# Late products with v on four tiles of TensorE instead of two, and whole copies of their probabilities

## The chip, the cores and the metric

One core of a Trainium2 chip. The metric is the device time of one execution in microseconds (us). The kernel before takes 708.42 us, the median of three runs (708.2 to 708.72). The engines are named as in the profile: PE is TensorE, PEld its weight loads, DVE is VectorE, ACT is ScalarE, POOL is GpSimd, SP is SyncE, which issues most of the transfers.

## The reference

Chunked attention with 8 memory keys, then a gated feed-forward on all tokens. Batch 4, 8 heads, 768 tokens, head size 64; chunks of 32 queries, each with 8 memory keys and 16 + 32 + 8 keys around it.

```python
for c in range(nc):
    k_full = np.concatenate([mem_k, k[:, :, l_start:r_end]], axis=2)   # 8 + up to 56 keys
    v_full = np.concatenate([mem_v, v[:, :, l_start:r_end]], axis=2)
    scores = scale * np.matmul(q_c, k_full.transpose(0, 1, 3, 2))
    scores = scores - np.max(scores, axis=-1, keepdims=True)
    a = np.exp(scores)
    a = a / (np.sum(a, axis=-1, keepdims=True) + 1e-09)
    out[:, :, c_start:c_end] = np.matmul(a, v_full)
...
rms = np.sqrt(np.mean(x * x, axis=-1, keepdims=True) + 1e-06)
xn = x / rms * rms_g
g = xn @ w_gate
silu = g * (1.0 / (1.0 + np.exp(-g)))
val = xn @ w_val
return (silu * val @ w_out).astype(np.float32)
```

x has 3072 tokens of 512 values (all heads side by side); the feed-forward is 1536 wide.

## The kernel before

**Blocks and units.** The tokens are worked in 8 blocks of 384 (half a batch element). A unit of attention is a block and a pair of heads: 12 chunks of 32 queries for two heads, 32 units in all. The first 8 units (early) and the first two blocks' feed-forward follow an order written out by hand. The other 24 units (late) are worked in 12 pairs, in between the feed-forward of the blocks ahead of them.

**The feed-forward.** For each of 12 slices f of the width, TensorE computes `pg` (gate) and `pv` (value) in 12 matmuls each, and then `po` (out) of the slice before in 9. Each product is made in three passes, with high and low parts of both operands (`xh`, `xl`, `hh`, `hl`, `wh`, `wl`). ScalarE does tanh (L451) and the cast `hh` (L162), VectorE the rest of the gating (L446, L455, L458) and `hl` (L467). TensorE's feed-forward matmuls of the late part stay in the order in which they are written, and so do the matmuls of the visits.

**Visits.** After `pg` or after `pv` of certain slices, given by a table, a visit (`late_steps`) issues attention work. A visit knows a pair `old`, whose probabilities are ready, and a pair `cur`, whose scores are to be made:

- `pT`: three transposes of 128x128 for each unit of `old` (`stage_p`), into two different banks of PSUM
- the copies of `pT` into `pt` (even unit) and `qp` (odd unit) in SBUF (`stage_c`)
- `s`: the scores of `cur` (`stage_s2`), tiles of 64 rows by 32 columns, for two units
- max, subtraction (VectorE), exponential (ScalarE) of `cur`
- `o`: the products of `old` with v (`stage_o`), then copies into `xT` and squares `sq` on ScalarE, their sum on VectorE (`late_r`)
- in every second visit the norm of a block begins (`late_n`): `sh` and `sl`, high and low part of the sum of squares, and later `ssum`, two matmuls with ones
- sums, reciprocals and products with `r` for `cur` (`stage_d`), which make the probabilities of the next visit's `old`

In the first block with visits, the step with `ssum` stands right after the next `pg`; in the later blocks a `pv` and more lie between. Parts of the visits have high priority and the scheduler sets the order on VectorE and ScalarE from there; each engine then works in that fixed order.

**Chunks and rows.** v is laid out with 128 rows for a pair of chunks: 64 keys of the even chunk, then 64 of the odd one. A transposed tile of probabilities has the same rows. Each row half is a chunk's keys, and its columns are that chunk's queries only. The kernel before wants one matmul with all 128 rows for the queries of both chunks, 64 columns, so each row half needs zeros in the columns of the other chunk: the tiles `pt` and `qp` are 768 wide, zeroed once by POOL (L122), and the copies write each row half to its own columns only. They are therefore four copies of 64x384 for a pair of units, two by ScalarE for the lower rows, two by VectorE for the upper.

Of the kernel before, what the change touches and what calls it, by code (L numbers as in the profile page):

```python
# [8 lines left out]
F32 = mybir.dt.float32  # L9
# [4 lines left out]
AF = mybir.ActivationFunctionType  # L14
ALU = mybir.AluOpType
# [5 lines left out]
CH = 32  # L21
# [3 lines left out]
P = 128  # L25
NG = H // 2
HT = 384
NT = HT // P
NC = HT // CH
NJ = NC // 2  # L30
# [4 lines left out]
NE = NG * 2  # L35
WP = 2 * KC - LC - RC
KN, VN = NJ * WP, NJ * 2 * D
# [33 lines left out]
def tile_kernel(ctx: ExitStack, tc: tile.TileContext, q, k, v, w_gate, w_val, w_out, rms_g, out):  # L71
    nc = tc.nc
    const = ctx.enter_context(tc.tile_pool(name="const", bufs=1))
    p1 = ctx.enter_context(tc.tile_pool(name="p1", bufs=1))
# [28 lines left out]
    def on_pe(ins):  # L103
        if pinned:
            tc.keep_in_program_order(ins)

    def psum_a(name):
        return psa.tile([P, 512], F32, name=name, tag="at")

    def psum_m(tag, name):  # L110
        return psm.tile([P, 512], F32, name=name, tag=tag)
# [4 lines left out]
    units = [(b, hf, g) for b in range(B) for hf in range(2) for g in range(NG)]  # L116
    st = {}
    pts = [early.tile([P, NT, 4, 2, CH], F32, name=f"pt{i}") for i in range(2)]
    late = {}

    def zeros(t):
        nc.gpsimd.memset(t, 0.0)  # L122
        return t

    def late_buffers(i):

        if i:
            t = p1.tile([P, HT + VN], F32, name="qp1", tag="A")
            late["q", 1], late["pt", 1] = t[:, 0:HT], zeros(t[:, HT:])
            late["kv", 1] = p1.tile([P, KN + VN], F32, name="kv1", tag="B")  # L130
        else:
            late["q", 0] = p1.tile([P, HT], F32, name="q0", tag="q")
            late["pt", 0] = zeros(p1.tile([P, VN], F32, name="pt0", tag="wy"))
            late["kv", 0] = p1.tile([P, KN + VN], F32, name="kv0", tag="ws")
        late["pt", i] = late["pt", i].rearrange("p (i a s q) -> p i a s q", i=NT, a=4, s=2)

    def load_qk(u):
        d = st.setdefault(u, {})
        if u < NE:
            d["q"] = early.tile([P, HT], F32, name=f"q{u}", tag=f"q{u % 6}")  # L140
            t = early.tile([P, KN], F32, name=f"k{u}", tag=f"k{u % 6}")
            nc.sync.dma_start(out=d["q"], in_=q[u])
        else:

            t = late["kv", u % 2][:, 0:KN]
            d["q"] = late["q", u % 2]
            nc.sync.dma_start(out=d["q"], in_=q[u])
        d["k"] = t.rearrange("p (j k) -> p j k", j=NJ)
        nc.sync.dma_start(out=t, in_=k[u])
# [5 lines left out]

    def pt_of(u):

        return pts[u % 2] if u < NE else late["pt", u % 2]

    def copy(e, out, in_):  # L160
        if e == "a":
            return nc.scalar.copy(out, in_)  # L162
        if e == "g":
            return nc.gpsimd.tensor_copy(out=out, in_=in_)
        return nc.vector.tensor_copy(out=out, in_=in_)  # L165
# [22 lines left out]
    def stage_s2(pair):  # L188

        for u in pair:  # L190
            st[u]["s"] = psum_a(f"s{u}")
        for i in range(NT):
            for cp in range(2):
                for par in range(2):
                    c, o = 4 * i + 2 * par + cp, (2 * i + cp) * KC
                    for u in pair:
                        d = st[u]
                        for e in range(2):
                            r, a = slice(64 * e, 64 * e + 64), 64 * par + CH * (e ^ u % 2)
                            on_pe(nc.tensor.matmul(d["s"][a:a + CH, o:o + KC], lhsT=d["q"][r, c * CH:c * CH + CH],  # L200
                                                   rhs=d["k"][r, c // 2, 40 * cp:40 * cp + KC], start=True, stop=True))

    def stage_m(u):
        stage_ma(u)
        stage_mb(u)
# [20 lines left out]
    def stage_e(u):  # L226
        pe = st[u]["p"]
        nc.scalar.activation(pe, pe, AF.Exp, scale=0.125)

    def stage_d(u):  # L230
        stage_da(u)
        stage_db(u)
# [25 lines left out]
    def stage_p(u, tag=None):  # L258
        d = st[u]
        t = psum_m(tag, f"pT{u}") if tag else psum_a(f"pT{u}")  # L260
        pe = d["p"].rearrange("p j k -> p (j k)")
        for i in range(NT):
            on_pe(nc.tensor.transpose(out=t[:, i * P:(i + 1) * P], in_=pe[:, i * P:(i + 1) * P], identity=ident))  # L263
        d["t"] = t

    def stage_c(u):
        stage_ch(u, 0, "a")
        stage_ch(u, 1, "d")

    def stage_ch(u, hh, e):  # L270
        r = slice(64 * hh, 64 * hh + 64)
        t4 = st[u]["t"][:, 0:HT].rearrange("p (i a q) -> p i a q", i=NT, q=CH)
        copy(e, pt_of(u)[r, :, :, hh, :], t4[r])

    def stage_o(u, tag=None):

        pt, vw = pt_of(u), st[u]["v"]
        o = psum_m(tag, f"o{u}") if tag else psum_a(f"o{u}")
        for j in range(NJ):
            for hh in range(2):  # L280
                on_pe(nc.tensor.matmul(o[64 * hh:64 * hh + 64, j * D:(j + 1) * D], lhsT=vw[:, j, hh],  # L281
                                 rhs=pt[:, j // 2, 2 * (j % 2) + (hh ^ (u % 2 if u >= NE else 0))].rearrange("p c q -> p (c q)"),
                                 start=True, stop=True))
        st[u]["o"] = o[:, 0:HT]

    def late_r(u, x):

        g = units[u][2]
        o = st.pop(u)["o"]
        nc.scalar.copy(x[:, g], o)  # L290
        s = obuf(f"sq{u}")[:, 0:HT]
        nc.scalar.activation(s, x[:, g], AF.Square)
        if g:
            nc.vector.tensor_tensor(out=s, in0=s, in1=late["ss"], op=ALU.add)
        late["ss"] = s

    def late_n(x):

# [191 lines left out]
    def obuf(name):  # L490
        return p3.tile([P, DM], F32, name=name, tag="stg")
# [59 lines left out]
    def last_of(eng):  # L551
        return next(i for i in reversed(nc.cur_bb.bb.instructions) if i.engine == eng.engine)
# [3 lines left out]
    def late_steps():  # L556


        pairs = [(u, u + 1) for u in range(NE, len(units), 2)]
        for n in range(len(pairs) + 1):  # L560
            old = pairs[n - 1] if n else ()
            cur = pairs[n] if n < len(pairs) else ()
            new = pairs[n + 1] if n + 1 < len(pairs) else ()
            for u in old[0:1]:
                if u % NG == 0:
                    late_x["x"] = p1.tile([P, NKT, HT], F32, name="xT", tag="x")
            x = late_x.get("x")
            with tc.high_priority():
                for i, u in enumerate(old):
                    stage_p(u, None if i else "g")  # L570
                for u in old:
                    stage_c(u)
            if not cur:
                yield "p"
            with tc.high_priority():
                if cur:
                    stage_s2(cur)
                for u in cur:
                    stage_m(u)
                for u in cur:  # L580
                    stage_e(u)
                for i, u in enumerate(old):
                    stage_o(u, "v" if cur and i else None)
                for u in old:
                    late_r(u, x)
            norm = late_n(x) if n and n % 2 == 0 else ()
            if norm:
                with tc.high_priority():
                    next(norm)
            with tc.high_priority():  # L590
                for i, u in enumerate(cur):
                    if norm and i:
                        with tc.issue_after(last_of(nc.vector)):
                            stage_d(u)
                    else:
                        stage_d(u)
            for u in new:
                load_qk(u)
            for u in cur if n else ():
                load_v(u)  # L600
            yield "v"
            for _ in norm:
                yield "n"

    def tok_R(n):
        late_buffers(0)
        load_qk(NE)
        load_v(NE)
# [5 lines left out]
    sq = [xq[:, i] for i in range(4)]  # L614
# [35 lines left out]
    def tok_in(w):  # L650
        def fn(n):
            b, f = SEQ[n]
            sp[w, n] = moe_in(w, f, xs01[b])
        return fn
# [28 lines left out]
    def tok_o(n):  # L683
# [10 lines left out]
        P=lambda n: stage_p(n, "o0" if n < NG else None),  # L694
# [4 lines left out]
        g=tok_in("g"), v=tok_in("v"), p=tok_q("g"), q=tok_q("v"),  # L699
        r=tok_r, h=tok_h, i=tok_i, j=tok_j, k=tok_k, l=tok_l, o=tok_o,  # L700
# [5 lines left out]
    for tok in ORDER.split():  # L706
# [4 lines left out]
        e = tok[-1] if tok[1:] and tok[-1].isalpha() else ""  # L711
# [41 lines left out]
    for sg, (blk, f0) in enumerate(segments):  # L753
# [7 lines left out]
        for f in range(f0, NF):  # L761
            g = moe_in("g", f, xs, last)
# [17 lines left out]
            else:  # L780
                with tc.high_priority():
                    t = moe_t(g, vv, blk)
# [70 lines left out]
```

## Time and profile before

| | |
|---|---|
| median of the runs | 708.42 us |
| profiled execution | 707.74 us |
| its span, first to last instruction | 705.9 us |
| TensorE clock granted, mean | 0.992 |
| PE busy | 687.4 us (97%) |
| DVE, ACT, POOL busy | 392.3, 261.4, 6.1 us |
| `o` of the late units, 12 pairs | first at 172.3 us, last at 605.8 us |

A row of a view in order of time gives the start, the length, the engine, the line of the kernel, the operation, its result and operands, shapes, and how many records it groups; in brackets stand the idle time ahead of it on its engine and what ended that. A matmul's length counts its whole way through the array, and the next begins well before it ends, so the pace of TensorE is read from starts. A matmul of 32-bit values leaves two records.

### The profile page before, as it was taken

To read this page: it belongs to the slowest core of one execution; us is meant where nothing else is said; L and a number is where in the kernel's file an instruction comes from. 1 tells how busy PE (TensorE), PEld (TensorE's weight loads), DVE (VectorE), ACT (ScalarE), POOL (GpSimd) and SP (SyncE) were. 2 spreads that over 40 slices of the span, in tenths; PEclk is the share of its full clock that TensorE was granted. 3 is DMA by queue.
4 is the path that set the end of the run, shared out by engine and by line. 5 is a ranking of instruction groups with operands and counts; after the bars stand their busy time and mean duration, and the time that the engine had idled before them with its cause. 6 is when DMAs were issued, how large, how long until landed. Compare 5 with 4: busy or idle time off the path is not lost.

```text
span 705.9 us, 13419 instructions
## 1 busy us (share of the span) xinstructions
PE 687.4 (97%) x5702; PEld 636.3 (90%) x5702; DVE 392.3 (56%) x780; ACT 261.4 (37%) x474; POOL 6.1 (1%) x14
## 2 busy tenths in 40 slices
PE   7899999999999999999999999999999999999997
PEld 6798898999989999999999999999999999999996
DVE  6789999857674327552383525735276532552222
ACT  4697987733333113331233313222133311331112
POOL 0010000000000000000000000000000000000000
PEclk8899999999999999999999999999999999999999
DMA  9644644333321103130021303013031100010001
GB/s 319 246 167 137 235 149 139 115 132 109 115 90 51 58 0 105 46 104 1 17 90 45 105 1 89 16 46 105 1 104 46 45 3 0 1 46 1 0 1 46
DMA packets 22620, 55.14 MB, mean 78 GB/s; under 512 B 2464, under 2 KB 6816, under 8 KB 22560
## 3 DMA queue, kind: packets, MB, share of 16 engines
q1 hardware_dynamic: 19824, 49.55, 20.9%
q10 hardware_dynamic: 2736, 4.72, 1.8%
q8 instruction: 45, 0.74, 0.5%
q14 instruction: 15, 0.12, 0.1%
HBM read 47.97 MB, written 6.29 MB: 77 GB/s over the span
## 4 chain that ended last, share of the span: by engine, by line
PE 88%; DVE 5%; ACT 4%; issue 1%; DMA 1%; POOL 0%; SPq 0%; DVEq 0%; ACTq 0%
PE pg L437 27%; PE pv L437 27%; PE po L487 27%; PE o L281 3%; PE pT L263 1%; ACT pt L162 1%; DVE pt L165 1%; DVE qp L165 1%; DMA k<-in_k_dram 1%; ACT ws L392 1%; ACT ws L381 1%; PE s L184 1%; PE ss L622 1%; ACT wy L382 1%; DVE xT L325 1%
## 5 line engine op out<-in xcount | busy, mean ns | idle before, releaser
L437 PE MATMUL pv<-xh,wh_v 128*128 128x384 f32 x384 | 130.1, 339 | 2.1 <-DVE t L458 2.1
L437 PE MATMUL pg<-xh,wh_g 128*128 128x384 f32 x384 | 130.5, 340 | 0.0
L437 PE MATMUL pv<-xh,wl_v 128*128 128x384 f32 x384 | 129.7, 338 | 0.5 <-DVE wl_v L408 0.5
L437 PE MATMUL pg<-xl,wh_g 128*128 128x384 f32 x384 | 129.8, 338 | 0.0
L437 PE MATMUL pg<-xh,wl_g 128*128 128x384 f32 x384 | 129.8, 338 | 0.0
L437 PE MATMUL pv<-xl,wh_v 128*128 128x384 f32 x384 | 129.6, 337 | 0.0
L162 ACT CAST hh<-t 128x384 fp32r<-128x384 f32 x89 | 45.8, 515 | 192.7 <-PE po L487 176.0
L487 PE MATMUL po<-wh_o,hh 128*128 128x512 f32 x285 | 113.9, 400 | 0.7 <-ACT hh L744 0.6
L487 PE MATMUL po<-wh_o,hl 128*128 128x512 f32 x285 | 112.6, 395 | 0.0
L487 PE MATMUL po<-wl_o,hh 128*128 128x512 f32 x285 | 112.3, 394 | 0.0
L455 DVE SCALAR_TENSOR_TENSOR t<-t,pg 128x384 f32<-128x384 f32 x72 | 39.9, 554 | 105.8 <-ACT t L451 105.7
L467 DVE TENSOR_TENSOR hl<-t,hh 128x384 fp32r<-128x384 f32 x89 | 49.5, 556 | 85.7 <-ACT hh L162 85.6
L458 DVE TENSOR_TENSOR t<-t,pv 128x384 f32<-128x384 f32 x95 | 52.7, 554 | 71.5 <-PE pv L437 70.2
L451 ACT ACTIVATE t<-pg 128x384 f32<-128x384 f32 x72 | 35.5, 493 | 120.2 <-PE pg L437 120.2
L437 PEld LDWEIGHTS pg<-xh,wh_g 128*128 128x128 f32 x384 | 72.3, 188 | 4.1 <-DVE gr L446 0.4
L437 PEld LDWEIGHTS pg<-xl,wh_g 128*128 128x128 f32 x384 | 72.3, 188 | 3.6
L437 PEld LDWEIGHTS pv<-xh,wh_v 128*128 128x128 f32 x384 | 72.0, 188 | 3.6 <-DVE t L458 1.8
L437 PEld LDWEIGHTS pv<-xh,wl_v 128*128 128x128 f32 x384 | 72.0, 188 | 0.8 <-DVE wl_v L408 0.8
L437 PEld LDWEIGHTS pg<-xh,wl_g 128*128 128x128 f32 x384 | 72.2, 188 | 0.0
L437 PEld LDWEIGHTS pv<-xl,wh_v 128*128 128x128 f32 x384 | 72.1, 188 | 0.1
L487 PEld LDWEIGHTS po<-wh_o,hl 128*128 128x128 f32 x285 | 53.6, 188 | 13.6 <-DVE hl L745 0.6
L487 PEld LDWEIGHTS po<-wh_o,hh 128*128 128x128 f32 x285 | 53.5, 188 | 10.7 <-ACT hh L744 1.6
(110 smaller groups left out, 717.2 us busy)
## 6 DMA issues: line engine op xcount, KB each, us to landing
kv<-in_v_dram SPq DMA_DIRECT2D x24, 384.0 KB, 5.6
kv<-in_k_dram SPq DMA_DIRECT2D x24, 312.0 KB, 4.2
out_dram<-ob ACTq DMA_DIRECT2D x18, 256.0 KB, 2.1
ws<-in_moe_w_gate_dram SPq DMA_DIRECT2D x4, 1024.0 KB, 4.9
ws<-in_moe_w_val_dram SPq DMA_DIRECT2D x4, 1024.0 KB, 5.0
ws<-in_moe_w_out_dram SPq DMA_DIRECT2D x4, 1024.0 KB, 5.0
q<-in_q_dram SPq DMA_DIRECT2D x20, 192.0 KB, 3.1
vw<-in_v_dram SPq DMA_DIRECT2D x8, 384.0 KB, 7.3
```

The lines of the kernel that those rows point to most:

```text
L162: return nc.scalar.copy(out, in_)
L165: return nc.vector.tensor_copy(out=out, in_=in_)
L184: nc.tensor.matmul(s[a:a + CH, o:o + KC], lhsT=d["q"][r, c * CH:c * CH + CH], rhs=k[r], start=True, stop=True)
L263: on_pe(nc.tensor.transpose(out=t[:, i * P:(i + 1) * P], in_=pe[:, i * P:(i + 1) * P], identity=ident))
L281: on_pe(nc.tensor.matmul(o[64 * hh:64 * hh + 64, j * D:(j + 1) * D], lhsT=vw[:, j, hh], rhs=pt[:, j // 2, 2 * (j % 2) + (hh ^ (u % 2 if u ...
L325: nc.vector.scalar_tensor_tensor(out=x[:, kt], in0=x[:, kt], scalar=rg[:, kt:kt + 1], in1=r, op0=ALU.mult, op1=ALU.mult)
L437: on_pe(nc.tensor.matmul(ps[:, 0:HT], lhsT=weight(a, n, f, kt), rhs=xs[c][:, kt], start=kt == 0 and i == 0, stop=kt == NKT - 1 and i == 2))
L451: nc.scalar.activation(t, g, AF.Tanh, scale=0.5)
L455: nc.vector.scalar_tensor_tensor(out=t, in0=t, scalar=1.0, in1=g, op0=ALU.add, op1=ALU.mult)
L458: nc.vector.tensor_tensor(out=t, in0=t, in1=vv, op=ALU.mult)
L467: nc.vector.tensor_tensor(out=hl, in0=t, in1=hh.bitcast(F32), op=ALU.subtract)
L487: on_pe(nc.tensor.matmul(po[i], lhsT=h[a][:, i * P:(i + 1) * P], rhs=weight(c, "o", f), start=f == 0 and n == 0, stop=f == NF - 1 and n == 2))
```

## The change

For the late units, the products with v are made for each row half by itself. The row half of the even chunks writes one bank of PSUM (`oe`), that of the odd chunks another (`oo`), both units of the pair side by side in each: 48 matmuls of 64 rows with 32 moving columns in place of 24 with 128 rows and 64 columns. No zeros are needed, so `pt` and `qp` are 384 wide, and one copy of 128x384 serves a unit, by ScalarE for the even and by VectorE for the odd one. The copies into `xT` take both units from one bank, and write pieces of 32 columns, every other chunk.

```diff
     def late_buffers(i):
         if i:
-            t = p1.tile([P, HT + VN], F32, name="qp1", tag="A")
-            late["q", 1], late["pt", 1] = t[:, 0:HT], zeros(t[:, HT:])
+            t = p1.tile([P, 2 * HT], F32, name="qp1", tag="A")
+            late["q", 1], late["pt", 1] = t[:, 0:HT], t[:, HT:]
...
     def stage_c(u):
-        stage_ch(u, 0, "a")
-        stage_ch(u, 1, "d")
+        copy("da"[u % 2 == 0], late["pt", u % 2], st[u]["t"][:, 0:HT])
...
+    def stage_o2(pair, tag):
+
+        st["o2"] = o2 = [psum_a(f"oe{pair[0]}"), psum_m(tag, f"oo{pair[0]}") if tag else psum_a(f"oo{pair[0]}")]
+        for j in range(NJ):
+            for n, u in enumerate(pair):
+                pt = late["pt", u % 2].rearrange("p (j e q) -> p j e q", j=NJ, e=2)
+                for cp in range(2):
+                    r, o = slice(64 * cp, 64 * cp + 64), (NJ * n + j) * CH
+                    for hh in range(2):
+                        on_pe(nc.tensor.matmul(o2[cp][64 * hh:64 * hh + 64, o:o + CH], lhsT=st[u]["v"][r, j, hh],
+                                               rhs=pt[r, j, hh ^ u % 2], start=True, stop=True))
+
+    def late_r(pair, x):
+
+        g = units[pair[0]][2]
+        o2 = st["o2"]
+        for u in pair:
+            st.pop(u)
+        xc = x[:, g:g + 2].rearrange("p g (j c q) -> p g j c q", c=2, q=CH)
+        for cp in range(2):
+            nc.scalar.copy(xc[:, :, :, cp], o2[cp][:, 0:HT].rearrange("p (g j q) -> p g j q", g=2, q=CH))
+        for i in range(g, g + 2):
+            s = obuf(f"sq{i}")[:, 0:HT]
+            nc.scalar.activation(s, x[:, i], AF.Square)
+            if i:
+                nc.vector.tensor_tensor(out=s, in0=s, in1=late["ss"], op=ALU.add)
+            late["ss"] = s
...
-                for i, u in enumerate(old):
-                    stage_o(u, "v" if cur and i else None)
-                for u in old:
-                    late_r(u, x)
+                if old:
+                    stage_o2(old, "v" if cur else None)
+                    late_r(old, x)
```

The written order of a visit stays, and TensorE's order is the one before but for the products. The scheduler's order on VectorE and ScalarE changes in the visits. On VectorE, in the visit at 187 us (the first with a norm), from the first sum for the softmax of `cur` to the norm's `sl`, before (`pe` are the probabilities, `r` their sums and reciprocals, `sq` the sums of squares of `old`):

```order
L250 TENSOR_REDUCE r_2271<-pe_2225 128x6
L294 TENSOR_TENSOR sq_2260<-sq_2260,sq_2050 128x384
L251 TENSOR_SCALAR r_2271<-r_2271 128x6
L252 RECIPROCAL r_2271<-r_2271 128x6
L256 TENSOR_TENSOR pe_2225<-pe_2225,r_2271 128x384
L246 MEMSET pe_2229 64x8
L294 TENSOR_TENSOR sq_2264<-sq_2264,sq_2260 128x384
L250 TENSOR_REDUCE r_2277<-pe_2229 128x6
L467 TENSOR_TENSOR hl<-t,hh 128x384
L251 TENSOR_SCALAR r_2277<-r_2277 128x6
L302 TENSOR_TENSOR sl<-sq_2264,sh 128x384
```

and in the changed kernel, where the same work stands at L245 to L251 and L305 to L313:

```order
L246 TENSOR_SCALAR r_2313<-r_2313 128x6
L247 RECIPROCAL r_2313<-r_2313 128x6
L251 TENSOR_TENSOR pe_2243<-pe_2243,r_2313 128x384
L241 MEMSET pe_2247 64x8
L245 TENSOR_REDUCE r_2319<-pe_2247 128x6
L246 TENSOR_SCALAR r_2319<-r_2319 128x6
L247 RECIPROCAL r_2319<-r_2319 128x6
L251 TENSOR_TENSOR pe_2247<-pe_2247,r_2319 128x384
L305 TENSOR_TENSOR sq_2303<-sq_2303,sq_2070 128x384
L305 TENSOR_TENSOR sq_2306<-sq_2306,sq_2303 128x384
L313 TENSOR_TENSOR sl<-sq_2306,sh 128x384
L478 TENSOR_TENSOR hl<-t,hh 128x384
```

Both additions of squares, which stood between the steps of the two softmax units, now stand behind them, `sl` behind them in turn, and `hl` behind `sl`. The four later visits with a norm and a `cur` change in the same way.

On ScalarE in the same visit, before, from the copies of `pT` on:

```order
L162 COPY pt_1716<-pT_2161 64x12x32
L162 COPY qp_1740<-pT_2165 64x12x32
L290 COPY xT<-o_2233 128x384
L228 ACTIVATE pe_2225<-pe_2225 128x384
L292 ACTIVATE sq_2260<-xT 128x384
L290 COPY xT<-o_2246 128x384
L228 ACTIVATE pe_2229<-pe_2229 128x384
L292 ACTIVATE sq_2264<-xT 128x384
L162 CAST hh<-t 128x384
L301 CAST sh<-sq_2264 128x384
```

and in the changed kernel:

```order
L157 COPY pt_1716<-pT_2181 128x384
L223 ACTIVATE pe_2243<-pe_2243 128x384
L223 ACTIVATE pe_2247<-pe_2247 128x384
L300 COPY xT<-oe_2251 128x12x32
L300 COPY xT<-oo_2252 128x12x32
L303 ACTIVATE sq_2303<-xT 128x384
L303 ACTIVATE sq_2306<-xT 128x384
L312 CAST sh<-sq_2306 128x384
L157 CAST hh<-t 128x384
```

The exponentials of both units come ahead of the copies of the products, and `sh` ahead of `hh`.

More of the change, by code (lines that the diff above doesn't have):

```diff
@@ L119, in tile_kernel @@
     late = {}
-    def zeros(t):
-        nc.gpsimd.memset(t, 0.0)
-        return t
     def late_buffers(i):
         if i:
-            t = p1.tile([P, HT + VN], F32, name="qp1", tag="A")
-            late["q", 1], late["pt", 1] = t[:, 0:HT], zeros(t[:, HT:])
+            t = p1.tile([P, 2 * HT], F32, name="qp1", tag="A")
+            late["q", 1], late["pt", 1] = t[:, 0:HT], t[:, HT:]
             late["kv", 1] = p1.tile([P, KN + VN], F32, name="kv1", tag="B")
@@ L132, in late_buffers @@
             late["q", 0] = p1.tile([P, HT], F32, name="q0", tag="q")
-            late["pt", 0] = zeros(p1.tile([P, VN], F32, name="pt0", tag="wy"))
+            late["pt", 0] = p1.tile([P, HT], F32, name="pt0", tag="wy")
             late["kv", 0] = p1.tile([P, KN + VN], F32, name="kv0", tag="ws")
-        late["pt", i] = late["pt", i].rearrange("p (i a s q) -> p i a s q", i=NT, a=4, s=2)
     def load_qk(u):
@@ L156, in pt_of @@
     def pt_of(u):
-        return pts[u % 2] if u < NE else late["pt", u % 2]
+        return pts[u % 2]
     def copy(e, out, in_):
@@ L281, in stage_o @@
                 on_pe(nc.tensor.matmul(o[64 * hh:64 * hh + 64, j * D:(j + 1) * D], lhsT=vw[:, j, hh],
-                                 rhs=pt[:, j // 2, 2 * (j % 2) + (hh ^ (u % 2 if u >= NE else 0))].rearrange("p c q -> p (c q)"),
+                                 rhs=pt[:, j // 2, 2 * (j % 2) + hh].rearrange("p c q -> p (c q)"),
                                  start=True, stop=True))
         st[u]["o"] = o[:, 0:HT]
[L286 to L295, printed above, removed]
+    def stage_o2(pair, tag):
[22 more added lines that the diff above has]
+            late["ss"] = s
     def late_n(x):
```

## The prediction

> **What bounds the kernel now.** I read the page's busy shares first, then who TensorE waited for, then the instructions in order of time around one visit.
>
> ```profile
> PE 687.4 (97%) x5702; PEld 636.3 (90%) x5702; DVE 392.3 (56%) x780; ACT 261.4 (37%) x474; POOL 6.1 (1%) x14
> ```
> ```profile
> PE o L281 <- DVE qp L165: 2.3, 11, 0.3
> PEld o L281 <- DVE qp L165: 4.1, 11, 0.4
> PEld ssum L306 <- DVE sl L302: 0.5, 1, 0.5
> ```
>
> TensorE (PE, with PEld for its weight loads) is busy all through, the other engines are not: time comes only from work on TensorE or from its waits. The second fence (who waited for whom between 150 and 640 us: total us, times, longest) shows one wait that recurs, 11 times: the late products `o` wait for the last copy of transposed probabilities by VectorE. One visit in order of time (start, length; `x` counts records, and a 32-bit matmul leaves two, so 24 are 12 matmuls):
>
> ```profile
> 170.12 0.82 PE L263 MATMUL pT<-ident,pe 128*128 128x128 f32 x6
> 170.71 0.47 ACT L162 COPY pt<-pT 64x384 f32<-64x384 f32 x1 [1.33 <-PE pT L263]
> 170.87 0.25 PE L200 MATMUL s<-kv,q 64*32 64x64 f32 x2
> 170.88 0.25 PE L200 MATMUL s<-kv,qp 64*32 64x64 f32 x2
> 171.08 0.47 ACT L162 COPY qp<-pT 64x384 f32<-64x384 f32 x1
> 171.21 0.56 DVE L165 COPY pt<-pT 64x384 f32<-64x384 f32 x1 [0.33 <-ACT pt L162]
> 171.69 0.55 DVE L165 COPY qp<-pT 64x384 f32<-64x384 f32 x1
> 171.81 0.23 PE L200 MATMUL s<-kv,qp 64*32 64x64 f32 x2
> 172.30 0.92 PE L281 MATMUL o<-pt,kv 128*64 128x64 f32 x24 [0.26 <-DVE qp L165]
> 173.05 0.87 PE L281 MATMUL o<-qp,kv 128*64 128x64 f32 x24
> 173.85 0.50 PE L487 MATMUL po<-wh_o,hh 128*128 128x512 f32 x1
> ```
>
> TensorE has its last `s` under way at 171.83 (the group's second record, 0.02 after its first) and starts `o` at 172.30, when the VectorE copy of 171.69 is done. VectorE could not begin earlier than 171.21, because it waits for ScalarE's half of the same tile.
>
> **The copies.** Four half copies become two whole ones, one on each engine, of different tiles. ScalarE's half takes 0.47 and a copy of 128x384 from PSUM costs it no more (`xT<-o`, below, 0.48); VectorE's takes 0.55. ScalarE would still start at 170.71 and end near 171.2. VectorE starts when the second unit's transposes are done: their last starts at 170.12 + 0.82 - 0.27 = 170.67, is through at 170.94, plus 0.1 as ScalarE's start shows; so 171.04 to 171.6, before the last `s`. What is left between `s` and the product is the change of tile shape. Two such changes show its price: from `pT` to `s` 170.87 - 170.67 = 0.20, of which a transpose streams (0.82 - 0.27) / 5 = 0.11; from `o` to `po` 0.15 after the last start (173.05 + 0.87 - 0.22 = 173.70), of which 0.06 is stream (24 records in 0.70, two at a time). So 0.09 beyond the stream, and 0.15 from the last `s` to the product. Now it is 0.47 here, and in the ten other visits 0.42, as in this one (last `s` at 188.34):
>
> ```profile
> 188.32 0.23 PE L200 MATMUL s<-kv,qp 64*32 64x64 f32 x2
> 188.75 0.28 PE L281 MATMUL o<-pt,kv 128*64 128x64 f32 x2 [0.20 <-DVE qp L165]
> ```
>
> That is worth 0.32 once and 0.27 in each other visit where nothing else takes it. The last pair (`o` at 604.4) has no such wait.
>
> **The products.** 24 matmuls of 128 rows and 64 moving columns become 48 of 64 rows and 32 moving columns: a quarter of the work each, on four tiles of the array instead of two. By streaming alone the time would halve. But every matmul also loads 64 columns of weights, and there are twice as many loads. The price of a load is seen where only one column is moved:
>
> ```profile
> 21.34 0.74 PEld L622 LDWEIGHTS ss<-onef,xq 128*128 128x128 f32 x6
> ```
>
> (0.74 - 0.19) / 5 = 0.11 for 128 columns, hence 0.055 for 64. `o` already runs at 0.058 a record on each of its two tiles, where load (0.055) and stream are equal. With four tiles each of 24 records the load stays at 0.055: 23 x 0.055 + 0.02 = 1.29 to 23 x 0.058 + 0.02 = 1.36 from first to last, plus 0.03 stream and 0.09: 1.41 to 1.48 until `po`, against 173.85 - 172.30 = 1.55 now. I take 1.45: **0.10 saved**, not half. Nearest for four tiles in two row halves is `s`: 96 records from 170.87 to 171.83, 0.01 a record; that is the lower bound, 0.96 + 0.12 = 1.08, a saving of 0.47. The upper bound is that two row halves in the same columns load in turn: 48 x 0.055 + 0.12 = 2.76, a loss of 1.21. I lean on the middle since in `s` records for the two row halves of the same columns start 0.01 apart although a load of 32 columns should take 0.11 / 4 = 0.03.
>
> The Trainium skill ("TensorE: Matmul & The Clock Gate", section "Wait — 56ns, not 53.3ns?") says that start-to-start of matmuls never drops below about 25 ns, however few columns move. By that, an estimate, 96 records would take 2.4 us. This trace disagrees for tiles: `s` starts 96 in 0.96.
>
> **What it moves: the order on VectorE.** In the changed order both softmax units are finished before the sums of squares and `sl`; ScalarE does both exponentials before the `xT` copies, and `sh` before `hh`. In the first visit with a norm, at 187, `ssum` comes right after the next `pg`, and TensorE waits there already:
>
> ```profile
> 188.73 1.02 DVE L211 TENSOR_REDUCE mx<-s 128x6 f32<-128x384 f32 x2
> 189.67 1.01 DVE L223 TENSOR_TENSOR pe<-s,mx 128x384 f32<-128x384 f32 x2
> 189.72 0.48 ACT L290 COPY xT<-o 128x384 f32<-128x384 f32 x1 [1.71 <-PE o L281]
> 190.25 0.52 ACT L228 ACTIVATE pe<-pe 128x384 f32<-128x384 f32 x1
> 190.83 0.07 DVE L246 MEMSET pe<- 64x8 f32 x1 [0.15 <-ACT pe L228]
> 190.93 0.55 DVE L250 TENSOR_REDUCE r<-pe 128x6 f32<-128x384 f32 x1
> 191.87 0.17 DVE L251 TENSOR_SCALAR r<-r 128x6 f32<-128x6 f32 x1
> 192.07 0.19 DVE L252 RECIPROCAL r<-r 128x6 f32<-128x6 f32 x1
> 192.29 0.56 DVE L256 TENSOR_TENSOR pe<-pe,r 128x384 f32<-128x384 f32 x1
> 192.91 0.07 DVE L246 MEMSET pe<- 64x8 f32 x1
> 193.00 0.56 DVE L294 TENSOR_TENSOR sq<-sq,sq 128x384 f32<-128x384 f32 x1
> 193.60 0.51 ACT L301 CAST sh<-sq 128x384 fp32r<-128x384 f32 x1 [0.61 <-DVE sq L294]
> 194.48 0.55 DVE L302 TENSOR_TENSOR sl<-sq,sh 128x384 fp32r<-128x384 f32 x1
> 194.62 0.33 PE L306 MATMUL ssum<-sh,one 128*128 128x384 f32 x1
> 195.09 0.44 PE L306 MATMUL ssum<-sl,one 128*128 128x384 f32 x1
> ```
>
> Steps between starts: 0.58 where one 128x384 operation needs the one before (189.67 to 190.25), 0.47 where not (two in 1.02), 0.10 from a memset to the sum, 0.20 and 0.22 through the small ones, 0.62 from the product with `r` to the next memset, 0.60 from `sq` to `sh`. Now the changed order, on this clock. `mx` starts at 188.62 (the last `s` is through at 188.56). Then subtraction 189.56, exponential 190.14, memset 190.72, sum 190.82, `r` 191.40 and 191.60, product 191.82, memset 192.44, sum 192.54, `r` 193.12 and 193.32, product 193.54, first `sq` 194.01, second 194.59, `sh` 195.19, `sl` 195.75, done 196.30. The second `ssum` goes at about 196.36 instead of 195.09: **1.27 lost**, and this visit's own gains are swallowed by the wait. Behind `ssum` stand `pv` and everything after; `gr` and the norm chain on VectorE move along by the same amount, so I book nothing twice.
>
> Four later visits have more room: there a `pv` lies in between.
>
> ```profile
> 350.52 0.23 PE L200 MATMUL s<-kv,qp 64*32 64x64 f32 x2
> 359.12 0.34 PE L306 MATMUL ssum<-sl,one 128*128 128x384 f32 x1
> 359.29 0.40 PE L487 MATMUL po<-wh_o,hh 128*128 128x512 f32 x1
> ```
>
> The last `s` there is at 350.54, and TensorE now reaches the second `ssum` 8.58 later; by the change 8.58 - 0.27 - 0.10 = 8.21. `sl` is done 196.30 - 188.34 = 7.96 after the last `s` and releases it at 8.02. It holds with 0.2 to spare, the thinnest cover here; if it is gone, each 0.1 costs 0.4 in all. `hl`, behind `sl` on VectorE, is done 0.47 later, 8.43; the first `po` comes at 359.29 - 350.54 - 0.37 = 8.38, but `hl` is read only two matmuls of 512 columns after that.
>
> At nothing: two POOL memsets (0.74 each, POOL is busy 6.1 us of the span), less work on VectorE and ScalarE (two half copies a visit), the `xT` writes in pieces of 32 (ScalarE's copies into such pieces take the same 0.47), no DMA moved.
>
> **Sum.** Gaps -0.32 - 9 x 0.27 = -2.75; products -0.10 x 11 (ten visits and the last pair) = -1.10; `ssum` +1.27: **-2.58 us**. The profiled execution took 707.74 with a span of 705.9, 0.68 below the median of the runs: span 703.3, execution 705.2, median 708.42 - 2.58 = **705.8**.
>
> **Rivals.**
>
> 1. The products run as fast as `s`: -0.47 x 11 = -5.17 in place of -1.10, but TensorE then reaches the later second `ssum` at 8.58 - 0.27 - 0.47 = 7.84, 0.18 too early, four times: -2.75 - 5.17 + 1.27 + 0.7 = -5.9, **702.5**. For it: the same count of records on like tiles. Against: twice the weight columns.
>
> 2. The wait for `ssum` costs the clock. TensorE would arrive at 194.62 - 0.37 = 194.25 and find `sh` done at 195.70 and `sl` at 196.30: some 1.5 us idle, one matmul, then 0.4. Rows of stages (length, busy us of PE, PEld, DVE, ACT, POOL, then PEclk):
>
> ```profile
> 25.50:28.90 3.40, 2.10 (x15) 1.88 (x14) 2.35 (x6) 1.62 (x3) 0.00 (x0) 1.00 0.85 338
> 28.90:32.40 3.50, 3.50 (x32) 3.25 (x32) 0.87 (x2) 0.96 (x2) 0.00 (x0) 0.51 0.05 20
> 56.26:59.67 3.41, 1.90 (x9) 1.61 (x10) 3.31 (x6) 3.00 (x4) 0.00 (x0) 1.00 0.76 292
> 59.67:63.10 3.43, 3.43 (x18) 3.05 (x18) 3.27 (x6) 2.88 (x5) 0.00 (x0) 1.00 0.00 0
> ```
>
> After 1.3 us idle in a stage of 3.4 the clock was halved for the next; after 1.5 it was not. With about 1.9 idle it may be: half of 3.4 lost, -2.58 + 1.7 = -0.9, **707.5**. The Trainium skill (same page, "What's actually happening") lets the clock fall only after an idle window of some 3.4 us; the first pair of rows contradicts a full one. By that rule this rival would be nothing.
>
> 3. Slower: the loads of the two row halves take turns in the columns, 2.76 for the products: -2.75 + 1.21 x 11 + 1.27 = +11.8, **720.2**. It decides from 0.068 for four records on, where 11 x 0.13 eats up what gaps and `ssum` leave. For it: no row here has two row halves with loads of 64 columns. Against: the starts in `s`.
>
> 4. Records leave no closer than those of `o` do now, 0.70 / 24 = 0.029, however little each moves: 96 x 0.029 + 0.12 = 2.90 for the products, a loss of 1.35 in each, -2.75 + 14.9 + 1.27 = +13.4, **721.8**. Against: `s`, 0.01 a record. The floor in the Trainium skill that is weighed above is a mechanism of this kind.
>
> 5. It doesn't remove the wait, because VectorE's copy is held up past the last `s` (0.37 late would do): -1.10 + 1.27 = +0.2, **708.6**.
>
> **Chances.** Forecast 0.54; rivals 0.12, 0.14, 0.10, 0.04, 0.06. The forecast's own range, from 1.41 to 1.48 for the products and 0.4 either way for `ssum`, is 705.0 to 706.9. The range 702.0 to 708.0 holds the forecast and rivals 1 and 2: 0.80. The bound of 0.2% (1.4 us, what can be told from no change) lies at 707.0 and 709.8: faster 0.62 (forecast 0.50, rival 1), same 0.23 (rivals 2 and 5, the forecast's tail), slower 0.15.
>
> **What would show it.** In the changed profile: no wait of the products for a copy; 0.15 from the last `s` to them; 1.41 to 1.48 from there to `po` (1.08 is rival 1, 2.76 rival 3); one `ssum` wait of about 1.9 us in the first norm visit and none in the four later; PEclk 1.00 after it (0.5 is rival 2). I am wrong in the sign if the products take more than 1.68, and in the size if the later norm visits wait too.

## The result and the profile after

The changed kernel takes **717.25 us** (median of four runs, 716.69 to 720.73) against 708.45 (708.2 to 708.72) before: a ratio of 1.0134, 95% interval 1.0102 to 1.0167. Slower, where 705.8 was forecast. The profiled execution took 716.69 with a span of 714.9 (before 705.9) at a mean clock of 0.990 (0.992).

Start with what went as planned. A visit in which nothing happened beside it, the one at 187, in order of time (start, length, engine, line, operation): the last `s`, the first product, the last product, the next `po`.

```profile
188.96 0.23 PE L195 MATMUL s<-kv,qp 64*32 64x64 f32 x2
189.12 0.25 PE L289 MATMUL oe<-pt,kv 64*64 64x32 f32 x2
...
190.50 0.23 PE L289 MATMUL oo<-qp,kv 64*64 64x32 f32 x2
190.65 0.50 PE L498 MATMUL po<-wh_o,hh 128*128 128x512 f32 x1
```

The last `s` starts at 188.975 (second record of its row), the product 0.146 later: the wait for a copy is gone, in all 11 visits. The copies do what was said; the visit at 355 shows one on each engine at the same time, both done (at 355.92 and 356.33) before the first product at 356.76:

```profile
355.44 0.48 ACT L157 COPY pt<-pT 128x384 f32<-128x384 f32 x1 [1.96 <-PE pT L258]
355.77 0.56 DVE L160 COPY qp<-pT 128x384 f32<-128x384 f32 x1
356.76 0.25 PE L289 MATMUL oe<-pt,kv 64*64 64x32 f32 x2
```

The products take 1.38 from first to last start and 0.15 more to `po`, 1.53 in all against 1.55 before. Now who TensorE waited for between 150 and 640 us (total us, times, longest), and the page's lines of busy time and of the queue that brings instructions:

```profile
PEld oe L289 <- issue: 4.5, 5, 1.6
PE oe L289 <- issue: 3.9, 4, 1.5
PEld oo L289 <- issue: 2.9, 2, 1.8
PE oo L289 <- issue: 2.7, 2, 1.7
PEld ssum L317 <- ACT sh L312: 1.6, 1, 1.6
```
```profile
PE 690.5 (97%) x6278; PEld 639.3 (89%) x6278; DVE 387.9 (54%) x768; ACT 257.3 (36%) x462; POOL 4.6 (1%) x12
...
q8 instruction: 49, 0.80, 0.4%
```

The `ssum` wait is the one that was forecast. The four rows above it are new: in the middle of the products TensorE stands still, and "issue" says that no other engine and no transfer of data in the profile released it. (Weight loads and matmuls are listed apart, so most of these holes stand in a row of each kind.) The six places, in order of time (the bracket holds the idle time, which begins only when the last matmul has ended by the profile's account):

```profile
173.73 0.24 PE L289 MATMUL oo<-pt,kv 64*64 64x32 f32 x1 [1.04 <-issue]
...
230.24 0.19 PE L289 MATMUL oo<-qp,kv 64*64 64x32 f32 x1 [1.68 <-issue]
...
273.55 0.24 PE L289 MATMUL oe<-pt,kv 64*64 64x32 f32 x2 [0.37 <-issue]
...
315.81 0.24 PE L289 MATMUL oe<-pt,kv 64*64 64x32 f32 x2 [0.64 <-issue]
...
525.46 0.24 PE L289 MATMUL oe<-qp,kv 64*64 64x32 f32 x1 [1.47 <-issue]
...
568.56 0.19 PE L289 MATMUL oe<-qp,kv 64*64 64x32 f32 x1 [1.42 <-issue]
```

From start to start these holes are 1.26, 1.90, 0.59, 0.83, 1.68 and 1.64. In these visits the products take 2.66, 3.30, 1.99, 2.26, 3.14 and 3.18 from first to last in place of 1.38: **8.2 us** in all. Two of them cost more. Stages around the second (length, busy us of PE, PEld, DVE, ACT, POOL, PEclk, DMA share, GB/s):

```profile
227.50:231.00 3.50, 1.82 (x97) 1.66 (x97) 3.22 (x10) 1.09 (x3) 0.00 (x0) 0.98 0.49 134
231.00:234.50 3.50, 3.50 (x9) 2.78 (x10) 1.95 (x7) 1.75 (x4) 0.00 (x0) 0.53 1.00 342
234.50:238.00 3.50, 3.50 (x22) 3.46 (x21) 1.11 (x2) 1.01 (x2) 0.00 (x0) 1.00 0.14 54
```

For 3.4 us behind the hole the clock is halved: 9 matmuls in a stage where the next has 22. The same follows the hole at 566.92 (PEclk 0.50 from 568.80 to 572.20).

The time from one visit's first `pT` to the next's adds all this up. The columns are the visit, its distance to the next before and after, the difference, and what of it is explained by the products' own excess over 1.38:

| visit (after) | before | after | difference | excess of the products |
|---|---|---|---|---|
| 169.83 | 16.51 | 17.44 | +0.93 | 1.27 |
| 187.27 (`ssum`) | 37.02 | 38.31 | +1.29 | 0 |
| 225.58 | 41.70 | 44.81 | +3.11 | 1.92, clock halved |
| 270.39 | 41.87 | 42.23 | +0.36 | 0.61 |
| 312.62 | 41.62 | 42.29 | +0.67 | 0.88 |
| 354.91 | 41.91 | 41.60 | -0.31 | 0 |
| 396.51 | 41.62 | 41.23 | -0.39 | 0 |
| 437.74 | 41.91 | 41.60 | -0.31 | 0 |
| 479.33 | 41.62 | 41.23 | -0.39 | 0 |
| 520.57 | 41.91 | 43.38 | +1.47 | 1.76 |
| 563.94 | 41.62 | 44.48 | +2.86 | 1.80, clock halved |

The differences add up to +9.3; the first visit comes 0.3 earlier, the part behind the last takes as long as before: +9.0, the whole difference of the spans. Four undisturbed visits are 0.35 shorter on average, so the change does gain what it was to gain. Taking that 0.35 off, the two halved stages cost some 1.5 and 1.4. The bill: holes +8.2, clock +2.9, `ssum` +1.3, ten visits -3.5, together 8.9 of the 9.3.

### The profile page after: what moved, and what is told of

Its sections match the earlier page's. It is cut to its first block, busy times and chain, and to the rows that moved or that the text cites. A ratio compares the mean times of both kernels' runs of the same rounds, so it can differ in the third digit from the quotient of the medians.

```text
span 714.9 us, 14546 instructions
## 1 busy us (share of the span) xinstructions
PE 690.5 (97%) x6278; PEld 639.3 (89%) x6278; DVE 387.9 (54%) x768; ACT 257.3 (36%) x462; POOL 4.6 (1%) x12
## 4 chain that ended last, share of the span: by engine, by line
PE 70%; DVE 1%; issue 1%; ACT 0%
PE po L498 22%; PE pg L448 22%; PE pv L448 21%; PE oe L289 2%; PE s L195 1%; PE pT L258 1%; PE oo L289 1%; DVE xT L336 0%; PE ssum L317 0%; PE po L526 0%; ACT hh L754 0%; DVE t L466 0%; DVE t L469 0%; DVE sl L313 0%; DVE sq L305 0%
```

## The experiments

**The theories.** Counted through the trace from 0, loads, matmuls and TensorE's 68 waiting instructions together, every one of the six holes lies before a record whose number is 193 modulo 256. TensorE also has such a hole in the kernel before, in the first part of the program:

```profile
24.17 0.49 PE L622 MATMUL ss<-onef,xq 128*128 128x1 f32 x3
26.80 0.39 PE L622 MATMUL ss<-onef,xq 128*128 128x1 f32 x3 [2.13 <-issue]
```

Its number is 961, which is 193 modulo 256 again. The instruction queue's packets carry 16 KB each (0.80 MB in 49), and one for TensorE comes about every 256 of its records: 64 bytes a record. In all six visits such a transfer starts 2.2 to 2.5 us before TensorE goes on. The view of the transfers between 227 and 231 us shows one, in the eighth of 40 slices of 0.1 us (the first row has tenths of the busy share); TensorE stands from 228.34 to 230.24, and `q1` brings data:

```profile
DMA  0000000600000035967956321000994712698899
GB/s 0 0 0 0 0 0 0 164 0 0 0 0 0 0 108 154 215 169 246 292 200 246 123 77 62 15 31 31 100 150 75 75 25 50 225 300 349 349 449 399
...
q1 hardware_dynamic: 246, 0.45, 40.9%
q8 instruction: 1, 0.02, 1.7%
```

Its packet lasts 0.9 to 1.1 us in the six visits; what fills the 1.2 to 1.5 us from its end to the next record, the trace doesn't show. So **F**, the theory of supply: instructions come in blocks of 256; TensorE goes on past a border only when the next block is there, and where two borders fall into one visit, the 256 records between them are used up faster than a block comes. A visit has 12 + 192 + 192 = 396 records now (300 before) in 3.2 us. In the six visits the 256 took 1.6 to 1.9 us. In the visit at 187 there are two borders, too (1.66 us apart), but the transfer had begun at 187.20, 0.9 before the first. In that at 355 the borders are 3.0 us apart. The other three hold one border each. Before, three visits had two borders, 2.4 to 2.6 us apart, and no hole.

The rivals put the holes down to their place, and not to a count: to the transfers of k, q and v that run there, or to the new form of the products (four tiles, two banks, one copy each). They are **D** and its like in the expectations.

**Shift the count.** 32 tiny matmuls (128 records, half a block, results unused) ahead of the first visits, nothing else.

```diff
-D4 W9 P6 P7 F C6a ...
+D4 W9 X32 P6 P7 F C6a ...
...
+    def shift(n):
+        w = pmw[-1]
+        for i in range(n):
+            r, a = slice(64 * (i % 2), 64 * (i % 2) + 64), 32 * (i % 4)
+            nc.tensor.matmul(w[a:a + 32, 0:1], lhsT=zero[r, 0:32], rhs=zero[r, 0:1], start=True, stop=True)
```

> The changed kernel with 32 tiny matmuls more in the early part (32 matmuls = 64 weight loads and 64 matmul records = 128 records), before any late unit; nothing else differs. Theory F (fetch): TensorE's instructions come in blocks of 256, and a visit of the changed kernel runs 396 of them without a pause; where two block boundaries fall into one visit, the second block is not there yet. Counting from the start of a visit's transposes, the first boundary now stands at record 59, 40, 74, 47, 16, 245, 214, 187, 156, 129, 98 in the eleven visits (172 to 564 us), and those below about 140 stall, but for the second. 128 records more move it to 187, 168, 202, 175, 144, 117, 86, 59, 28, 1, 226: F expects stalls of 0.6 to 1.9 us in the 6th to 9th visit (about 354, 396, 437, 479 us), perhaps in the 10th, and none in the 1st to 4th and the 11th. Rival D (the data or the place: row halves, banks, the landing of v): the same six visits stall as before (172, 225, 270, 312, 520, 564), by the same amounts. Time by F 714 to 719 us, by D 717 to 718.

Measured 715.5 us (713.8 to 719.93), ratio to before 1.0112 (1.0082 to 1.0142). The holes moved to the other visits. The products at 229.76 ran through in 1.38; those that had run through now stand. Three rows, of the visits near 400 and 444 and of the waits:

```profile
401.85 0.25 PE L296 MATMUL oo<-pt,kv 64*64 64x32 f32 x2 [1.35 <-issue]
...
446.40 0.24 PE L296 MATMUL oo<-pt,kv 64*64 64x32 f32 x1 [1.69 <-issue]
```
```profile
PE oo L296 <- issue: 4.6, 4, 1.7
```

From start to start: 1.33 at 355.94, 1.57 at 400.27, 1.90 at 444.50, 0.62 at 489.31, and 0.96 at 314.26 in the `po` behind the products; none in the products of the six visits that stood before (the one at 314.26 falls just behind those of the fifth visit). The work, the tiles and the data transfers of each visit are what they were. That excludes every theory that goes by the place alone. The profiled execution, at 719.93, is the slowest of the four, and not by the holes alone: its first visit begins 3.95 later than in the changed kernel, with 20.5 us at half clock ahead of it in place of 6.8.

**Add only the count.** The kernel before with 24 tiny matmuls (96 records, results unused) between scores and products in each visit. Its copies, zeros and products are untouched.

```diff
+    def pad(pair):
+        for i in range(24):
+            u, e = pair[i // 2 % 2], i % 2
+            d, r, a = st[u], slice(64 * e, 64 * e + 64), 64 * (i // 4 % 2) + CH * (e ^ u % 2)
+            on_pe(nc.tensor.matmul(d["s"][a:a + CH, 480:481], lhsT=d["q"][r, 0:CH], rhs=d["k"][r, 0, 0:1],
+                                   start=True, stop=True))
...
+                    if old:
+                        pad(cur)
```

> The kernel before (zeros, 24 products of 128 rows), with 24 tiny matmuls more (64 rows, 32 columns of weights, 1 moving column; 96 records) between the scores and the products of each of the 11 visits, where TensorE waits 0.42 us for the copies anyway. They write unused columns of the score bank. F: the records of a visit become 396, at the same places in the instruction stream as in the changed kernel, so the same visits stall (172, 225, 270, 312, 520, 564; 0.5 to 1.9 us each) although tiles, copies and order are those of before: 713 to 720 us. D: it costs what the 48 records take beyond the wait, at most 0.2 a visit: 708.4 to 711 us, no stall.

Measured 721.13 us (717.08 to 722.47), ratio 1.0172 (1.0146 to 1.0198). Four of the six rows, in order of time, then a stage:

```profile
174.67 0.69 PE L289 MATMUL o<-pt,kv 128*64 128x64 f32 x17 [2.15 <-issue]
...
232.70 0.51 PE L289 MATMUL o<-pt,kv 128*64 128x64 f32 x10 [1.78 <-issue]
...
277.03 0.86 PE L289 MATMUL o<-pt,kv 128*64 128x64 f32 x22 [1.05 <-issue]
...
319.70 0.19 PE L208 MATMUL s<-kv,q 64*32 64x1 f32 x1 [0.72 <-issue]
```
```profile
233.90:237.30 3.40, 3.40 (x9) 2.68 (x9) 2.97 (x11) 1.96 (x5) 0.00 (x0) 0.51 0.95 347
```

The same six visits stand as in the changed kernel (from start to start 2.38, 2.00, 1.32, 0.88, 1.39, 1.41), here in products of the old form; the fourth, at 319.70, in the pads themselves. A seventh, the first with a norm, stands for 0.21 at 192.40. In visits without a hole the pads cost 0.1 to 0.2. So 96 more records per visit are enough for the whole loss, and the new form of the products is not needed for it. The time came out a little above what F expected.

**Thin the visits out.** The changed kernel with the products behind the `po` that follows, so that nine long matmuls stand between 192 and 192 short ones.

```diff
-VISITS = (((1, "v"), (5, "v"), (9, "v"), (10, "n"), (11, "n"), (12, "n")),
+VISITS = (((1, "v"), (5, "o"), (9, "o"), (10, "n"), (11, "n"), (12, "n")),
...
+            if old and cur:
+                yield "o"
             with tc.high_priority():
...
                 out_()
+                if steps.get(2 * (f - f0) + 1) == "o" and next(todo) != "v":
+                    raise AssertionError(f)
```

> The changed kernel with the same 48 products per visit, but issued after the po of that place instead of ahead of it, so that 9 matmuls of 512 columns (2.1 us, 18 records) stand between the scores and the products. F: no visit has 256 records in under 3 us any more, so no stall within the products and no halved clock behind them; each visit gains 0.27 (no wait for copies), loses 0.09 to one more change of tile shape, and ssum in the first norm visit still costs 1.27: 708.45 - 2.1 + 1.3 = about 707.6 us (706.8 to 708.4). D: the products stall as before in six visits, 715 us or more.

Measured 709.34 us (708.12 to 710.55), ratio 1.0013 (1.0003 to 1.0023). No hole in any product, where 256 records now take 3.7 to 4.0 us: 8 us came back by order alone, with the same instructions. The expected 707.6 was missed all the same. In the profiled execution, at 710.54, the first visit begins 1.18 later than before, and the first norm visit takes 40.19 against 37.02. Rows of it in order of time, and stages:

```profile
197.17 0.44 PE L317 MATMUL ssum<-sh,one 128*128 128x384 f32 x1 [1.43 <-ACT sh L312]
197.76 0.44 PE L317 MATMUL ssum<-sl,one 128*128 128x384 f32 x1 [0.15 <-DVE sl L313]
```
```profile
195.40:198.80 3.40, 1.81 (x9) 1.24 (x9) 2.67 (x7) 1.04 (x2) 0.00 (x0) 1.00 0.52 154
198.80:202.20 3.40, 3.40 (x12) 3.21 (x11) 2.37 (x5) 0.52 (x1) 0.00 (x0) 0.50 0.00 0
202.20:205.60 3.40, 3.40 (x19) 3.10 (x18) 2.29 (x6) 0.51 (x1) 0.00 (x0) 0.99 0.00 0
```

The wait for `sh` and then a halved stage: rival 2 of the prediction, in this execution. From visit to visit the split kernel takes 41.44 and 41.82, against 41.62 and 41.91 before and 41.23 and 41.60 in the undisturbed visits of the changed kernel: the split keeps 0.13 of the 0.35.

**Move the first block's visits.** The split kernel with the visits of the first block one slice earlier, so that the norm has time.

```diff
-VISITS = (((1, "v"), (5, "o"), (9, "o"), (10, "n"), (11, "n"), (12, "n")),
+VISITS = (((1, "v"), (3, "o"), (7, "o"), (10, "n"), (11, "n"), (12, "n")),
```

> e2_split, and the visits of the first block one slice earlier (after slices 1 and 3 of the block instead of 2 and 4), so that more than a slice lies between the first norm visit and ssum. If the wait at ssum is the order on VectorE and costs 1.27 us against before, it is gone, and the 0.3 that the kernel before waits there too: 1.6 us below e2_split, about 706.0 us (705.2 to 706.8). If it is not (the chain is needed at the end of the block instead), the same as e2_split.

Measured 708.16 us (706.08 to 709.34), ratio 0.9994 (0.9983 to 1.0005): missed by 2 us. The `ssum` wait is gone, but the earlier visit finds its probabilities not ready:

```profile
166.71 1.08 PE L258 MATMUL pT<-ident,pe 128*128 128x128 f32 x6 [1.54 <-DVE pe L251]
```

**Move the norm instead.** The split kernel with the three norm steps one place later, with the kernel before as a control, and with the shift of 128 records.

```diff
-... (9, "o"), (10, "n"), (11, "n"), (12, "n")),
+... (9, "o"), (11, "n"), (12, "n"), (13, "n")),
```

> The split kernel with the three norm steps of the first block one place later (after the pv that follows, where the later blocks have them). If the wait for ssum is all that the split kernel still loses (1.77 + 0.59 us less the ordinary 0.2 in its profile, and half a clock stage of up to 1.7 behind it), ssum no longer waits at 195, the clock stays at 1.0 behind it, and the time is 709.3 - 2.1 = 707.2 if the clock falls rarely, 705.6 if it falls in every execution: 706.4 (705.4 to 707.4), 2 us below the kernel before. If the split itself (issue order, phase of the instruction blocks) costs it, it stays at 708.5 to 709.5.

Measured 708.87 us (706.58 to 711.46), ratio 1.0013 (0.9995 to 1.0031): no gain. `ssum` does not wait, but the last `po` of the block waits longer: for `hh` 0.84 where it is 0.63 in the split kernel, and for `hl`, which queues behind the norm's last steps on VectorE and made no wait there, 1.31. In this execution, at 711.45, the clock is halved behind them, from 210.89 to 214.30:

```profile
208.29 0.50 PE L498 MATMUL po<-wh_o,hh 128*128 128x512 f32 x1 [0.84 <-ACT hh L757]
...
210.34 0.50 PE L498 MATMUL po<-wh_o,hl 128*128 128x512 f32 x1 [1.31 <-DVE hl L758]
```

> The kernel before with the same three norm steps one place later: a control, since a gain of the run above could come from the norm steps alone. Before loses 0.47 us to the second ssum in the first norm visit: 0.3 to 0.5 us faster, 708.1 (707.7 to 708.6). If it gains 2 us, the norm steps, not the late products, make the gain of the run above.

The control took 707.48 us (706.14 to 708.38; before 708.34 in these runs), ratio 0.9991 (0.9979 to 1.0003). That is a little below the range, but its gain isn't told apart from none, and it is no 2 us.

> The run with split visits and later norm steps, with 32 tiny matmuls (128 records, results unused) early on, so that the borders of the 256-instruction blocks move by half a block in every visit. Supply theory: with a po of 9 matmuls between scores and products no 256 records are consumed in under 2 us wherever the borders fall, so no stall of 0.5 us or more labelled issue in s or in the products, and the time is that of the unshifted run plus 0.0 to 0.8 (in the unsplit kernel the same 32 matmuls moved the stalls to other visits). If the split kernel escaped only by a lucky phase, stalls come back in some of the 11 visits: 3 us or more above the unshifted run.

Measured 710.5 us (707.04 to 712.5), ratio 1.0032 (1.0015 to 1.0049), 1.6 above the unshifted run, with intervals that overlap. The profiled execution has no hole at a border in any product. Its distances from visit to visit are the same within 0.1 but for the first norm visit, which takes 38.19 against 39.92, as no halved stage follows its waits. So the split does not live on a lucky count. But 1.6 is twice what was expected, and that execution (709.01) doesn't show where the others lost it; their mean clocks spread from 0.983 to 0.997. Open.

**Put both together.** By the theory the products may stand right behind the scores wherever the borders fall well. In the changed kernel that was so in the four visits from 355 to 480, and the count of records ahead of them is the same in the split kernel. So: four visits unsplit, the others split, the first block's visits early (the table now has a row for each block, and a visit with the letter "v" passes the added stop). Then the same with the 32 tiny matmuls, which must hit just these four.

```diff
-VISITS = (((1, "v"), (5, "o"), (9, "o"), (10, "n"), (11, "n"), (12, "n")),
-          ((5, "o"), (17, "o"), (19, "n"), (20, "n"), (21, "n")),
+VISITS = (((1, "v"), (3, "o"), (7, "o"), (10, "n"), (11, "n"), (12, "n")),
           ((5, "o"), (17, "o"), (19, "n"), (20, "n"), (21, "n")),
+          ((5, "o"), (17, "v"), (19, "n"), (20, "n"), (21, "n")),
+          ((5, "v"), (17, "v"), (19, "n"), (20, "n"), (21, "n")),
+          ((5, "v"), (17, "o"), (19, "n"), (20, "n"), (21, "n")),
           ((5, "o"), (17, "p"), (18, "v"), (20, "n"), (21, "n"), (22, "n")))
```

> Split visits and the earlier visits of the first block, but four visits (near 351, 393, 434 and 476 us) with the products right behind the scores again, in which the block borders by the trace of the changed kernel fell harmlessly; every TensorE instruction before them is counted the same. Supply theory: no stall in those four, and each takes 0.2 less from visit to visit than split (41.23 and 41.60 there in the changed kernel against 41.44 and 41.82), so 708.2 - 0.8 = 707.4 (706.6 to 708.2). If stalls belonged to unsplit visits whatever the count, some of the four would stall.

Measured **707.06 us** (706.02 to 709.2) against 709.35 (707.45 to 710.77) of the kernel before in these runs: ratio 0.9977 (0.9964 to 0.9989). No hole; the four visits take 41.60, 41.23, 41.62 and 41.36. This version beats the kernel before by a quarter of a per cent.

> The run above with 32 tiny matmuls (128 records, results unused) early on. Supply theory: the borders move by half a block, and the four unsplit visits are just those that stalled in the changed kernel with the same 32 matmuls (355.9, 400.3, 444.5, 489.3): all four stall, 1.33 + 1.57 + 1.90 + 0.62 us with three half clock stages behind them, which made the four intervals 2.97 + 3.22 + 3.44 + 0.71 = 10.3 longer; the split visits don't stall. 717 (713 to 719), against 707.4 without the shift. If the stalls have another cause, the 32 matmuls cost under 1 us.

Measured 718.75 us (716.15 to 720.85), ratio 1.0133 (1.0111 to 1.0156). All four stand, and no other: three rows, of the fourth the bracket is too short to be shown (0.58 from start to start, at 485.25).

```profile
358.31 0.25 PE L298 MATMUL oo<-pt,kv 64*64 64x32 f32 x2 [1.01 <-issue]
...
401.07 0.25 PE L298 MATMUL oo<-pt,kv 64*64 64x32 f32 x2 [1.08 <-issue]
...
443.86 0.24 PE L298 MATMUL oo<-pt,kv 64*64 64x32 f32 x1 [1.50 <-issue]
```

In this execution (716.15) the holes lengthened the four distances by 4.85 in all, and no stage behind them was halved; the others, up to 720.85, have a lower mean clock (0.980 to 0.985, against 0.987), as halved stages would give. The rest of its 7.7 above the span without the shift (714.4 against 706.7) lies ahead of the four: the first visit begins 1.56 later and takes 1.32 longer, with the clock halved from 169.47 to 172.89. The same 32 tiny matmuls that moved the split kernel by 1.6 us move this one by 11.7, the greater part of it by the four visits as far as this one trace shows.

## Why the prediction was wrong

**The gap, -2.75: right.** 0.146 from the last `s` to the products where 0.15 was forecast, in every visit; 0.27 saved in each, 0.33 in the first. Rival 5 falls by it.

**The products, -1.10: right in kind, mis-sized.** Not half the time and not twice: a round of four tiles takes 1.382 / 23 = 0.060 where the load of 64 columns was put at 0.055 to 0.058. The step "I take 1.45" measured 1.53, and 0.02 was saved instead of 0.10. Rivals 1, 3 and 4 (0.96, 2.64 and 2.78 from first to last) all fall by this number. From visit to visit 0.35 is gained all the same, near the forecast's 0.27 + 0.10; the 0.06 beyond gap and products I didn't locate.

**`ssum`, +1.27: right.** The second one comes 8.05 after the last `s` (8.02 forecast), the visit's distance grew by 1.29, and the four later norm visits don't wait.

```profile
196.43 0.44 PE L317 MATMUL ssum<-sh,one 128*128 128x384 f32 x1 [1.30 <-ACT sh L312]
197.02 0.44 PE L317 MATMUL ssum<-sl,one 128*128 128x384 f32 x1 [0.15 <-DVE sl L313]
```

**Rival 2, the clock behind that wait:** it didn't come in the changed kernel's profiled execution and did in the split one's, after a wait of 1.77 instead of 1.64. Its price, 1.7, was about right: the two stages behind holes cost 1.5 and 1.4.

**The step that failed** is the pricing of twice as many matmuls: "48 matmuls of 64 rows with 32 moving columns" got the terms stream, load and change of tile, and no term for bringing 96 more records a visit to the engine. That term is +8.2, and +2.9 through the clock, more than four times the forecast's gain. It stood in no rival either. Rival 4 asked how close records can follow each other and was answered by `s`, 0.01 a record; but `s` shows that only for 192 records at a time. The right question was for how long TensorE can keep that pace.

The trace of before had the answer within sight. I quoted the stages from 25.50 and 28.90 as evidence on the clock, and didn't ask what had made TensorE idle there: it was the hole at 24.17 to 26.80, "issue", in a stretch of short matmuls. A reading of that row, with one instruction packet of 16 KB for every 256 records, would have given an estimate: two borders in 396 records in about half of the visits (140 of 256 places), a block that is there some 2.5 us behind its start (24.27, for 26.80), some 1.7 us for 256 records at the new pace, hence some 0.8 us of standing still in such a visit if the transfer starts with the first border, and more if it starts later. The Trainium skill ("Runtime: NRT & Kernel Launch", section "Instruction fetch mechanics") does state the blocks of 16 KiB, 256 instructions each; but it calls the cost of crossing a border mostly hidden, since dispatch is slower than the fill. The runs agree on the blocks. On the cost the measurement decides: 0.6 to 1.9 us per crossing in the six visits, where TensorE runs through 256 records in under 2 us.

## What to carry to other kernels

Count instructions, not only their time: a stretch of TensorE with more than 256 records (a 32-bit matmul is two, its weight load two more) within 2 us can run out of instructions, and halving tiles doubles the records. The profile says it as idle time "issue" in the middle of a run of like instructions; whether it happens depends on the count of all TensorE instructions ahead, so an edit far away moves it, and shifting the count by 128 is the test for it. The remedy was to put long matmuls between two bursts of short ones; here it cost 0.2 us a visit, as the split kernel kept 0.13 of 0.35.

## What the runs showed of the hardware

- **A block border has a price.** TensorE went on 2.2 to 2.9 us after the start of the 16 KB transfer. With 256 records in 1.6 to 1.9 us it stood for 0.6 to 1.9 us, in the padded kernel up to 2.38, unless the transfer had begun early (187.20 before a border at 188.11). In the visits it never stood with 2.4 us or more; in between it went both ways (2.11 and 2.19 with a hole, 2.21 without). The early hole at 24.5 came although its 256 records had taken 3.95 us: its transfer started only at 24.18. So the start decides, and what sets it, in the seven visits with two borders within 2 us from 0.9 us before the first border to 1.3 behind it, is open; the trace shows no request for a block.
- **A hole can halve the clock.** After holes of 1.64 and 1.90 in the changed kernel the clock was 0.5 for 3.4 us, after one of 1.68 it was not; in the shifted one a hole of 1.33 was enough, in the mixed and shifted one 1.72 wasn't. The length alone doesn't decide. The place counts: in each trace the halved stages begin whole multiples of 3.413 us apart (in the changed kernel at 12.43, 46.56, 230.88 and 568.80, the last three 10, 64 and 163 of them behind the first). Points of this grid cut the hole of 1.68 (at 524.43, into 0.65 and 1.03) and that of 1.72 (at 442.54, into 0.39 and 1.32), while those of 1.64, 1.90 and 1.33 lie between two points. That isn't the whole rule: a hole of 1.41 between two points, at 573.47 in the padded kernel, was not followed by half clock.
- **Four tiles of 64x64 gave nothing over two of 128x64** for a product with few moving columns: 96 records in 1.38 us against 48 in 1.40. A round of four loads of 64 columns took 0.060, as long as one pair of loads with 128 rows.
